# Unused rows of r, k and w at the head of each half, set once on the chip; a dense first v; a newly planned order

## The chip, the core and the metric

The kernel runs on one core of one Trainium2 chip. The metric is device time in microseconds (us) of one execution; the median of several executions is compared. A profile was taken of one execution. Engines: TensorE (PE, weight loads as PEld), VectorE (DVE), ScalarE (ACT), GpSimd (POOL) and SyncE (SP), which issues the transfers.

## The reference

A recurrent attention layer feeds a two-layer product with a gate. Batch 4, 8 heads, 768 tokens, 48 values a head; 2,048 hidden values.

```python
for t in range(S):
    cur = np.einsum('bhd,bhe->bhde', u[None] * kt, vt)
    y[:, :, t] = np.einsum('bhd,bhde->bhe', rt, state + cur)
    state = wt[:, :, :, None] * state + np.einsum('bhd,bhe->bhde', kt, vt)
x = y as (B * S, 384)
h = x @ w_in
g = np.where(h >= 1, h, np.where(h <= -1, 0.0, (h + 1) ** 2 / 4))
out = g @ w_out
```

r, k, v are about 0.1 in size, w lies between 0.8 and 0.95.

## The kernel before, in words

**Attention** works in 12 units of 256 tokens, three for each batch entry, one after the other because a state passes along within an entry. Heads stand in pairs: one pair fills 128 rows, head h in rows 64h to 64h + 47; 16 rows of each half are unused and hold 0 for r and k and 1 for w. They come from DRAM with the rest (`rows` in `layouts`, L982: 128 rows for each load). For each unit `attention` (L384):

- loads w (`wq`, three buffers, 257.5 KB) and r with k (`rk`, three buffers, 512 KB) for two halves q, and v. Units 0 to 3 multiply k by u on chip; later units load r and k also by token (`nk`). A buffer of `rk` is free for the next load when the products of an earlier unit have read it.
- VectorE makes running products of w, forward (`p`, L439) and backward (`y`, L434), two scans each with 514 steps, and multiplies k by y (L468) and r by p (L518).
- TensorE makes the products of r with k among 64 tokens (`among`, L488); VectorE picks the valid part (L494); TensorE transposes k (L527), ScalarE copies it (`kt`, L534); TensorE makes the sums of k and v for each 64 tokens (`umat`, L549); VectorE adds them up into states (L565 to L570); TensorE makes the output of the unit from states and picked products (`cross` and `along`, L598). ScalarE and VectorE write it in two parts as `x`, and for heads that don't fit, six small transfers move rows (L700).
- Unit 0 is handled alone: its v comes from DRAM already spaced to 64 columns a head, into the gate's buffers `g0` and `g1` (256 KB each), and a permutation matrix (`perm`, 192 KB, from DRAM) takes the place of the small transfers.

**Weights** come as 16 packed blocks of 768 KB (`weight`, L343): ScalarE makes one half-word (L363) and the magnitude (L360), GpSimd the other half-word (L364), VectorE puts them together (L366), ScalarE rounds to a first part (L356), VectorE makes the second (L369).

**The two layers** (`products`, L745): for blocks of 512 tokens and each of 16 weight blocks, nine products for h (L952), ScalarE and VectorE for the gate (L763 to L768), nine products for the output (L972). Early steps take 256 tokens.

**The order** of all of it is written out by a planner (`Plan`): each operation has a due time, worked out from tables of numbers (`LEADS`, `DECODES`, `LOADS`, `RAWS`, `SLACK`) and the planner's own costs, and each engine's instructions are emitted in the order that comes out. Where it sees a gap on TensorE it adds products with zeros (`cleared`, L331).

At the start GpSimd sets constants and zeroes buffers (L306 to L318).

Of the kernel before, what the change touches and what calls it, by code (L numbers as in the profile page):

```python
# [13 lines left out]
AF = mybir.ActivationFunctionType  # L14
# [8 lines left out]
NU = NT // UT  # L23
# [25 lines left out]
class Plan:  # L49
# [16 lines left out]
    def __init__(self):  # L66
        self.ops, self.writer, self.readers = [], {}, {}

    def add(self, engine, cost, emit, due, reads=(), writes=(), port=False, size=0, fresh=True, mode=128, spare=0.0):
# [11 lines left out]
        deps.discard(n)  # L81
        self.ops.append(dict(e=engine, cost=cost, emit=emit, due=due, deps=deps, port=port, size=size,
                             fresh=fresh and engine == "PE", touch={*reads, *writes}, mode=mode, spare=spare))
        return n

    def group(self, first, when, lead, loads=0.0):
# [46 lines left out]
    def order(self):  # L133
# [13 lines left out]

        def opened(n):
            op = ops[n]
            since[n] = max((ran[m] if ops[m]["e"] == op["e"] and not ops[m]["size"] else end[m] + self.HOP for m in op["deps"]), default=0.0)  # L150
            open_[op["e"]].append(n)

        def ready(n):
# [62 lines left out]

SLACK = 0.759
LEADS = {0: 384.81, 1: 606.87, 2: 40.05, 3: 27.03, 4: 45.45, 5: 71.8, 6: 60.98, 7: 25.74, 8: 81.18, 9: 211.42, 10: 77.25, 11: 123.12}  # L220
# [12 lines left out]
ALONE = {0}  # L233
INPLACE = {0, 1}
SCALED = {0, 1}
STEP, FIRST, PACED, AFTER = 27.1568, 703.402, 25.4941, 8.52
ROUNDS = 6


def attention_moe(tc, a):  # L240
# [142 lines left out]

    def attention(u, when):  # L384
        if u == EARLY:
            load((when, 40.0), u_sb, a["us"], ["us"])
        first, due = len(plan.ops), None
        third = u % UB
        early = u < EARLY
# [63 lines left out]

        for q in (1, 0):
            s = slot[q]
            if early:
                if u in SCALED:
                    for pr in range(2):
                        op("ACT", 0.42, due, [("k", s), "cst"], [("ku", q), "nk"], lambda q=q, pr=pr: A.activation(
                            ku[:, q, pr * UT : pr * UT + UT], rk[slot[q]][:, 1, pr * UT : pr * UT + UT], AF.Copy,  # L460
                            scale=u_col[:, 2 * q + pr : 2 * q + pr + 1]))
# [515 lines left out]
def layouts(r, k, v, w, u, moe_w_in, moe_w_out):  # L977
# [12 lines left out]
    def tokens(x):  # L990
        return x.transpose(0, 2, 1, 3).reshape(NU, 2, 128, DM).transpose(0, 2, 1, 3)
# [23 lines left out]
    col[:, :D] = u.reshape(4, 2, D).transpose(1, 2, 0)  # L1015
    consts = np.concatenate([eye, two, col.reshape(128, 4)], axis=1)
    v0 = np.pad(tokens(v)[0].reshape(128, 2, H, D), [(0, 0)] * 3 + [(0, HP - D)]).reshape(128, 2, H * HP).transpose(1, 0, 2)
    perm = np.zeros((2, HP, 3, 2, HP), np.float32)
    for j in range(3):
        for h in range(2):  # L1020
            perm[h, 16 * j : 16 * j + 16, j, h, D:] = np.eye(16)
    perm = perm.reshape(128, 3 * 128)
    out = dict(nat=nat, v0=v0, perm=perm, rk=rk, w=rows(wz, 1.0), nk=nk, v=tokens(v), u=ul, wbits=wbits, consts=consts, below=below, us=us)
# [18 lines left out]
```

## Time and profile before

| | us |
|---|---|
| median of 3 runs | 511.38 (510.29 to 512.46) |
| profiled execution | 509.98 |
| its span, first to last instruction | 508.1 |
| TensorE busy | 492.1 |
| VectorE busy | 332.0 |
| ScalarE busy | 295.4 |
| GpSimd busy | 101.1 |

The profiled execution's own time is 1.9 us over its span, and 1.4 us under the median. A busy share is a mean over the whole span; matmuls are pipelined, so a busy TensorE is not TensorE at its peak. The granted clock of TensorE was 0.996 of full speed in the mean.

### The profile page before, as it was taken

How to read it: one execution, taken by the hardware profiler on the slowest of the kernel's cores; microseconds unless marked ns; L12 is line 12 of the kernel's file. 1: busy time of each engine (PE TensorE's matmuls, PEld its weight loads, DVE VectorE, ACT ScalarE, POOL GpSimd, SP SyncE). 2: the span in 40 equal slices, each digit the busy share in tenths (PEclk: the TensorE clock that was granted, in tenths of full speed). 3: DMA queues.
4: the chain of work that ended last, by engine and by line, in shares of the span. 5: the costliest groups of instructions: out<-in, count | busy, mean ns of one | idle time of the engine just before them, and what ended most of it. 6: DMA issues, size and time to landing. Idle time of an engine off the chain costs nothing.

```text
span 508.1 us, 13247 instructions
## 1 busy us (share of the span) xinstructions
PE 492.1 (97%) x5562; PEld 412.2 (81%) x5562; DVE 332.0 (65%) x561; ACT 295.4 (58%) x604; POOL 101.1 (20%) x68
## 2 busy tenths in 40 slices
PE   8999999999999999999999899999999999999994
PEld 7778987889999978888888687888878888888883
DVE  6899997947997799749646888842464333343331
ACT  3588798987876464746534565553463543454440
POOL 2487766801011212111002013000010000000000
PEclk9999999999999999999999999999999999999998
DMA  8974734326742334414006352200110000100001
GB/s 308 404 287 148 276 145 163 115 65 208 219 117 109 126 110 136 162 43 173 23 1 192 106 164 93 89 1 1 63 55 6 17 1 0 64 0 1 0 1 68
DMA packets 21923, 54.13 MB, mean 107 GB/s; under 512 B 3104, under 2 KB 8672, under 8 KB 21856
## 3 DMA queue, kind: packets, MB, share of 16 engines
q1 hardware_dynamic: 21856, 53.21, 30.8%
q8 instruction: 45, 0.74, 0.6%
q14 instruction: 22, 0.18, 0.1%
HBM read 46.32 MB, written 4.72 MB: 100 GB/s over the span
## 4 chain that ended last, share of the span: by engine, by line
PE 76%; DVE 13%; ACT 3%; DMA 3%; issue 3%; SPq 1%; DVEq 0%; ACTq 0%
PE h L952 34%; PE acc L972 33%; PE bank L598 4%; DVE y L434 2%; DVE r L494 2%; PE bank L488 2%; DVE wt L369 2%; DMA rk<-in_rk 1%; DVE p L439 1%; PE bank L527 1%; DMA wq<-in_w 1%; PE bank L549 1%; DVE g L765 1%; DVE gl L768 1%; DVE rk L518 1%
## 5 line engine op out<-in xcount | busy, mean ns | idle before, releaser
L952 PE MATMUL h<-x,wt 128*128 128x512 f32 (+1 forms) x1008 | 216.7, 361 | 1.1 <-DVE g L765 0.7
L952 PEld LDWEIGHTS h<-x,wt 128*128 128x128 f32 x1008 | 168.4, 188 | 30.6 <-DVE g L765 1.1
L972 PE MATMUL acc<-gh,wt 128*128 128x512 f32 (+1 forms) x672 | 151.7, 359 | 0.0
L972 PEld LDWEIGHTS acc<-gh,wt 128*128 128x128 f32 x672 | 113.8, 188 | 19.0
L765 DVE SCALAR_TENSOR_TENSOR g<-g,h 128x512 f32<-128x512 f32 (+1 forms) x112 | 67.4, 605 | 92.1 <-ACT g L764 85.0
L763 ACT ACTIVATE g<-h 128x512 f32<-128x512 f32 (+1 forms) x112 | 59.7, 533 | 85.3 <-PE h L952 84.9
L768 DVE TENSOR_TENSOR gl<-g,gh 128x512 fp32r<-128x512 f32 (+1 forms) x112 | 71.4, 642 | 28.6 <-ACT gh L767 13.4
L767 ACT CAST gh<-g 128x512 fp32r<-128x512 f32 (+1 forms) x112 | 62.1, 557 | 39.3 <-PE acc L972 17.8
L972 PE MATMUL acc<-gl,wt 128*128 128x512 f32 (+1 forms) x336 | 84.1, 357 | 0.0
L972 PEld LDWEIGHTS acc<-gl,wt 128*128 128x128 f32 x336 | 58.4, 187 | 9.8 <-DVE gl L768 0.4
L764 ACT ACTIVATE g<-g 128x512 f32<-128x512 f32 (+1 forms) x112 | 64.0, 571 | 3.2
L364 POOL TENSOR_SCALAR rr<-wraw 128x768 uint16<-128x768 f32 x16 | 52.7, 3293 | 34.8 <-DVE fl L366 17.2
L514 POOL TENSOR_TENSOR r<-cst,d 128x512 f32<-128x512 f32 x16 | 18.0, 1145 | 159.4 <-PE bank L598 134.0
L506 POOL TENSOR_TENSOR nk<-nk 128x768 f32<-128x768 f32 x8 | 16.9, 2108 | 80.3 <-DMA nk<-in_nk 71.2
L434 DVE TENSOR_TENSOR_SCAN y<-wq,seeds 128x514 f32<-128x514 f32 x24 | 32.2, 1342 | 0.8
L439 DVE TENSOR_TENSOR_SCAN p<-wq,seeds 128x514 f32<-128x514 f32 x24 | 30.2, 1259 | 3.5 <-POOL st L318 2.1
L468 DVE TENSOR_TENSOR rk<-rk,y 128x512 f32<-128x512 f32 x24 | 18.9, 789 | 3.5 <-DMA rk<-in_rk 3.3
L598 PEld LDWEIGHTS bank<-rk,st 48*48 48x48 f32 (+1 forms) x656 | 11.4, 121 | 9.3 <-DVE st L567 4.0
L369 DVE TENSOR_TENSOR wt<-fl,wt 128x768 fp32r<-128x768 f32 x16 | 16.4, 1032 | 3.2 <-ACT wt L356 3.1
L331 PE MATMUL bank<-clear 128*128 128x512 f32 (+1 forms) x57 | 16.8, 411 | 1.6 <-DVE seeds L438 1.6
L363 ACT ACTIVATE rr<-wraw 128x768 uint16<-128x768 uint32 x16 | 17.5, 1094 | 1.1 <-DVE fl L366 1.1
L518 DVE TENSOR_TENSOR rk<-rk,p 128x512 f32<-128x512 f32 x24 | 17.7, 748 | 0.1
(109 smaller groups left out, 384.3 us busy)
## 6 DMA issues: line engine op xcount, KB each, us to landing
rk<-in_rk SPq DMA_DIRECT2D x24, 512.0 KB, 4.8
wraw<-in_wbits SPq DMA_DIRECT2D x16, 768.0 KB, 7.5
wq<-in_w SPq DMA_DIRECT2D x24, 257.5 KB, 3.3
nk<-in_nk SPq DMA_DIRECT2D x8, 768.0 KB, 4.6
vn<-in_v SPq DMA_DIRECT2D x11, 384.0 KB, 5.9
fl<-in_w SPq DMA_DIRECT2D x12, 257.0 KB, 2.8
out_y<-g SPq DMA_DIRECT2D x11, 256.0 KB, 2.3
x<-last SPq DMA_DIRECT2D x66, 32.0 KB, 2.9
```

The costliest lines, as they stand in the source:

```text
L364: op("POOL", 3.35, due, [("raw", f)], ["rr_high"], lambda: G.tensor_scalar(out=r16[:, :, 1], in0=wraw[f][:, :, 1].bitcast(F32), scalar1=0. ...
L369: op("DVE", 0.95, due, [("fl", k), ("wh", f)], [("wl", f)], lambda: V.tensor_tensor(out=w_lo[f], in0=s, in1=w_hi[f].bitcast(F32), op=ALU.s ...
L434: V.tensor_tensor_scan(out=y_[:, ::-1], data0=w[:, SEG:0:-1], data1=sv[:, ::-1], initial=0.0, op0=ALU.mult, op1=ALU.add)
L439: V.tensor_tensor_scan(out=pv[:, q].rearrange("p n c -> p (n c)"), data0=w[:, 0:SEG], data1=sv, initial=0.0, op0=ALU.mult, op1=ALU.add,)
L598: PE.matmul(out=bank[by[g]][HP * half : HP * half + wide, lo : lo + C], start=first, stop=False, skip_group_check=True, **kw)
L763: op("ACT", c, due, [("b", 6 + hk)], [("g", gk)], lambda: nc.scalar.activation(gs, hs, AF.Relu, scale=0.5, bias=0.5))
L764: op("ACT", c, due, (), [("g", gk)], lambda: nc.scalar.activation(gs, gs, AF.Square))
L765: op("DVE", 0.13 + 0.56 * k, due, [("b", 6 + hk)], [("g", gk)], lambda: nc.vector.scalar_tensor_tensor(out=gs, in0=gs, scalar=1.0, in1=hs, ...
L767: op("ACT", c, due, [("g", gk)], [("gh", gk)], lambda: nc.scalar.copy(ghs, gs))
L768: op("DVE", 0.18 + 0.52 * k, due, [("g", gk), ("gh", gk)], [("gl", gk)], lambda: nc.vector.tensor_tensor(out=gls, in0=gs, in1=ghs.bitcast( ...
L952: nc.tensor.matmul(by16(hp, f), lhsT=wx[f][:, cs], rhs=by16(xt[:, j, :], f), start=n == 0, stop=n == 8)
L972: nc.tensor.matmul(by16(o[j]), lhsT=wx[f][:, cs], rhs=by16(gt), start=first and i == 0, stop=stop and i == 2, skip_group_check=True)
```

## The change

The 16 unused rows of each half move to its head: head h now stands in rows 64h + 16 to 64h + 63. For units 0 to 6 the loads of w and of r with k begin at row 16 and have 112 rows (225 and 448 KB); rows 0 to 15 of the buffers are set once on the chip, before the first use (`unread`, `PADS`; the rows 64 to 79 still come with the load). Units 7 to 11 load all 128 rows. Products that read 48 rows of a half or 48 columns of k now take 64. The v of unit 0 comes dense (384 KB) into `vn0` and ScalarE copies it into the spaced `g0` and `g1`, which GpSimd has zeroed. The permutation matrix is made by GpSimd from the identity. The load of u for unit 4 waits for the last weight. All numbers of the order are new.

```diff
+PAD = HP - D
+PADS = [(0, "w", "DVE", (0, 199.0)), (1, "w", "ACT", (0, 190.0)), (0, "k", "POOL", (0, 198.0)), (1, "k", "POOL", (0, 196.0)),
+        (2, "w", "POOL", (0, 194.0)), (2, "k", "POOL", (0, 192.0))]
+WHOLE, MOST, TWO = ((0, 128),), ((PAD, 128),), ((PAD, HP), (HP + PAD, 128))
+CUT = [{"w": MOST, "k": MOST}, {"w": MOST, "k": MOST}, {"w": WHOLE, "k": WHOLE}]
...
-SLACK = 0.759
+SLACK = 1.82
...
+    for c2 in range(2):
+        op("POOL", 0.5, LATER, (), [("g", c2)], lambda c2=c2: G.memset(g_[c2], 0.0))
...
+    def unread(s, what, how, when):
+        t, v, keys = (wq[s], 1.0, [("w", s)]) if what == "w" else (rk[s], 0.0, [("k", s), ("r", s)])
...
+                op(how, 0.55 if what == "w" else 1.04, when, (), [(*keys[0], i)], lambda i=i: e.memset(t[i : i + PAD], v))
...
-            load((when, 40.0), u_sb, a["us"], ["us"])
+            load((when, 40.0), u_sb, a["us"], ["us"], [("wl", NF // 2)])
...
-            load(due, wq[slot[q]], a["w"][u, q], [("w", slot[q])])
-            load(due, rk[slot[q]], a["rk"][u, q], [("k", slot[q]), ("r", slot[q])])
+                cut = CUT[0 if u == 0 else 1 if u <= GUARDED else 2]["w" if t is wq[slot[q]] else "k"]
+                n = None
+                for i, j in cut:
+                    n = load(due, t[i:j], of[i:j], keys, twin=n)
...
-                load(due, g_[c2], a["v0"][c2], [("g", c2)])
-            load(due, perm, a["perm"], ["perm", "nk"])
+                op("ACT", 0.48, due, [("v", 0)], [("g", c2)], lambda c2=c2: A.copy(
+                    g_[c2].rearrange("p (h e) -> p h e", e=HP)[:, :, 0:D], v[:, c2, 0:DM].rearrange("p (h e) -> p h e", e=D)))
+            op("POOL", 0.4, due, (), ["perm", "nk"], lambda: G.memset(perm, 0.0))
+            op("POOL", 0.3, due, ["cst"], ["perm"], lambda: G.tensor_copy(
...
-                            i, o = slice(HP * g, HP * g + HP), slice(HP * h, HP * h + D)
+                            i, o = slice(HP * g, HP * g + HP), slice(HP * h, HP * h + HP)
...
-            i = slice(HP * h, HP * h + D)
+            i = slice(HP * h, HP * h + HP)
```

**SyncE at the start**, before: unit 0's last loads, unit 1's, then the first weight block. (Names end in a buffer's number; `in_wbits` are weights, `wq1`, `wq2`, `rk2`, `vn1` there are unit 1's or 2's.)

```order
L301 DMA rk1_83<-in_rk 128x1024
L301 DMA g0_104<-in_v0 128x512
L301 DMA g1_105<-in_v0 128x512
L301 DMA below0_71<-in_below 128x64
L301 DMA wq2_81<-in_w 128x515
L301 DMA rk2_84<-in_rk 128x1024
L301 DMA vn1_87<-in_v 128x2x384
L301 DMA wq0_79<-in_w 128x515
L351 DMA wraw0_229<-in_wbits 128x1536
```

The same place in the change:

```order
L309 DMA rk1_83<-in_rk 112x1024
L309 DMA vn0_86<-in_v 128x2x384
L309 DMA below0_71<-in_below 128x64
L379 DMA wraw0_206<-in_wbits 128x1536
L309 DMA wq2_81<-in_w 112x515
L309 DMA rk2_84<-in_rk 112x1024
L309 DMA vn1_87<-in_v 128x2x384
L379 DMA wraw1_220<-in_wbits 128x1536
```

The first weight block stands ahead of unit 1's loads, and the second right behind them.

**VectorE in unit 0**, before: from the second k multiply to the first pick (r multiplies L518, scans of unit 1 L439 and L434).

```order
L468 TENSOR_TENSOR rk1_83<-rk1_83,y0_89 128x512
L518 TENSOR_TENSOR rk0_82<-rk0_82,p0_88 128x512
L438 MEMSET seeds0_73 128x2
L439 SCALAR_TENSOR_TENSOR p0_88<-wq2_81,seeds0_73 128x514
L433 RECIPROCAL seeds0_73<-p0_88 128x2
L434 SCALAR_TENSOR_TENSOR y0_89<-wq2_81,seeds0_73 128x514
L518 TENSOR_TENSOR rk1_83<-rk1_83,p0_88 128x512
L438 MEMSET seeds0_73 128x2
L439 SCALAR_TENSOR_TENSOR p0_88<-wq0_79,seeds0_73 128x514
L565 COPY ob0_113<-h1_121 128x4x48
L567 TENSOR_TENSOR ob0_113<-bank2_124,ob0_113 128x4x48
L494 COPY_PREDICATED r0_91<-cst0_67,acc0_117 128x512
```

The same place in the change:

```order
L506 TENSOR_TENSOR rk1_83<-rk1_83,y0_89 128x512
L556 TENSOR_TENSOR rk0_82<-rk0_82,p0_88 128x512
L556 TENSOR_TENSOR rk1_83<-rk1_83,p0_88 128x512
L532 COPY_PREDICATED r0_91<-cst0_67,acc0_117 128x512
L532 COPY_PREDICATED r1_92<-cst0_67,acc1_118 128x512
L475 MEMSET seeds0_73 128x2
L476 SCALAR_TENSOR_TENSOR p0_88<-wq2_81,seeds0_73 128x514
L603 COPY ob0_113<-h1_121 128x4x48
L605 TENSOR_TENSOR ob0_113<-bank2_124,ob0_113 128x4x48
L605 TENSOR_TENSOR g2_106<-h1_121,ob0_113 128x4x48
L532 COPY_PREDICATED r0_91<-below0_71,acc2_119 128x512
L394 SCALAR_TENSOR_TENSOR fl0_114<-fl0_114,rr0_116 128x768
```

Unit 0's two r multiplies and its first picks stand ahead of unit 1's first scan; unit 1's second scan and the first scan of its other half are moved behind the state adds, and the first weight is put together there (L394).

**SyncE ahead of unit 8**, before (`rk2` is unit 8's second half, `rk0` unit 9's first, `x1` the small transfers of units 6 and 7):

```order
L700 DMA x1_102<-last0_103 16x2x256 x4
L301 DMA wq1_80<-in_w 128x515
L301 DMA wq2_81<-in_w 128x515
L301 DMA rk0_82<-in_rk 128x1024
L301 DMA vn1_87<-in_v 128x2x384
L301 DMA rk2_84<-in_rk 128x1024
L700 DMA x1_102<-last0_103 16x2x256 x6
```

The same place in the change:

```order
L738 DMA x1_102<-last0_103 16x2x256 x6
L309 DMA wq1_80<-in_w 128x515
L309 DMA wq2_81<-in_w 128x515
L309 DMA nk0_85<-in_nk 128x1536
L309 DMA rk2_84<-in_rk 128x1024
L309 DMA rk0_82<-in_rk 128x1024
L309 DMA vn1_87<-in_v 128x2x384
L738 DMA x1_102<-last0_103 16x2x256 x6
```

Unit 8's `rk2` stands ahead of unit 9's `rk0` and of the v load.

## Rows read from the trace of the kernel before

**Rows 1.** The page's part 1: busy time, share of the span, instructions of each engine.
```profile
PE 492.1 (97%) x5562; PEld 412.2 (81%) x5562; DVE 332.0 (65%) x561; ACT 295.4 (58%) x604; POOL 101.1 (20%) x68
```

**Rows 2.** Stretches: length, busy PE, PEld, DVE, ACT, POOL, clock, DMA share, GB/s.
```profile
12.00:14.00 2.00, 2.00 (x69) 1.77 (x70) 1.93 (x3) 0.19 (x1) 0.00 (x0) 1.00 1.07 426
...
40.00:60.00 20.00, 19.01 (x362) 17.41 (x363) 19.85 (x31) 15.70 (x35) 16.77 (x8) 1.00 0.69 245
60.00:80.00 20.00, 19.66 (x155) 16.91 (x157) 19.69 (x32) 18.60 (x34) 10.56 (x5) 1.00 0.43 158
...
180.00:200.00 20.00, 19.28 (x273) 15.86 (x272) 19.16 (x31) 10.60 (x25) 5.24 (x3) 1.00 0.44 146
...
250.00:300.00 50.00, 48.04 (x689) 38.17 (x688) 32.36 (x57) 24.84 (x53) 6.50 (x5) 1.00 0.31 103
```

**Rows 3.** VectorE's timeline: start, length, what, idle time before and its releaser.
```profile
3.62 1.23 DVE L439 TENSOR_TENSOR_SCAN p<-wq,seeds 128x514 f32<-128x514 f32 x1 [2.09 <-POOL st L318]
...
10.73 0.69 DVE L518 TENSOR_TENSOR rk<-rk,p 128x512 f32<-128x512 f32 x1
...
11.84 1.23 DVE L439 TENSOR_TENSOR_SCAN p<-wq,seeds 128x514 f32<-128x514 f32 x1 [0.40 <-DMA wq<-in_w]
...
14.45 0.67 DVE L518 TENSOR_TENSOR rk<-rk,p 128x512 f32<-128x512 f32 x1
...
17.03 1.36 DVE L494 COPY_PREDICATED r<-cst,acc 128x512 f32<-128x512 int32 x2
...
22.28 0.96 DVE L369 TENSOR_TENSOR wt<-fl,wt 128x768 fp32r<-128x768 f32 x1 [0.90 <-ACT wt L356]
24.57 0.96 DVE L366 SCALAR_TENSOR_TENSOR fl<-fl,rr 128x768 int32<-128x768 int32 x1 [1.33 <-POOL rr L364]
...
35.18 0.40 DVE L765 SCALAR_TENSOR_TENSOR g<-g,h 128x256 f32<-128x256 f32 x1
```

**Rows 4.** The same view, GpSimd and TensorE.
```profile
0.87 0.53 POOL L306 MEMSET seeds<- 128x514 f32 x1
...
16.73 3.06 POOL L364 TENSOR_SCALAR rr<-wraw 128x768 uint16<-128x768 f32 x1 [13.17 <-DMA wraw<-in_wbits]
...
25.61 3.56 POOL L364 TENSOR_SCALAR rr<-wraw 128x768 uint16<-128x768 f32 x1 [1.08 <-DVE fl L366]
...
27.04 1.57 PE L952 MATMUL h<-x,wt 128*128 128x256 f32 x9
```

**Rows 5.** The same view near 184 us: GpSimd and VectorE side by side.
```profile
183.77 2.08 POOL L506 TENSOR_TENSOR nk<-nk 128x768 f32<-128x768 f32 x1 [10.08 <-DMA nk<-in_nk]
...
184.27 2.66 DVE L434 TENSOR_TENSOR_SCAN y<-wq,seeds 128x514 f32<-128x514 f32 x1
```

**Rows 6.** Around unit 8: chain (start, length), timeline, and a stretch as in rows 2.
```profile
265.70 1.56 PE bank L598 x96
...
267.95 7.52 DMA rk<-in_rk
...
266.14 0.33 SPq L301 DMA_DIRECT2D rk<-in_rk  x1
...
278.77 2.31 DVE L518 TENSOR_TENSOR rk<-rk,p 128x512 f32<-128x512 f32 x1
...
280.00:282.00 2.00, 0.87 (x57) 0.87 (x60) 1.95 (x3) 0.00 (x0) 0.53 (x1) 1.00 0.46 133
```

**Rows 7.** Chain: products of L488; stretches, PE alone: L549, then L598 (64 and 48 wide).
```profile
302.54 1.09 PE bank L488 x64
...
184.00:185.20 1.20, 0.94 (x64) 1.00 0.01 3
...
41.00:44.00 3.00, 1.63 (x96) 1.00 0.39 79
86.00:88.00 2.00, 1.56 (x96) 1.00 0.17 37
```

**Rows 8.** Timeline of SyncE's issues: the loads ahead of unit 9.
```profile
294.97 0.82 SPq L301 DMA_DIRECT2D rk<-in_rk  x2
```

More of the change, by code (lines that the diff above doesn't have):

```diff
@@ L67, in __init__, with add @@
         self.ops, self.writer, self.readers = [], {}, {}
-    def add(self, engine, cost, emit, due, reads=(), writes=(), port=False, size=0, fresh=True, mode=128, spare=0.0):
+    def add(self, engine, cost, emit, due, reads=(), writes=(), port=False, size=0, fresh=True, mode=128, spare=0.0, twin=None):
         deps = {self.writer[x] for x in (*reads, *writes) if x in self.writer}
@@ L81, in add @@
         deps.discard(n)
+        if twin is not None:
+            deps = {*self.ops[twin]["deps"], twin}
         self.ops.append(dict(e=engine, cost=cost, emit=emit, due=due, deps=deps, port=port, size=size,
-                             fresh=fresh and engine == "PE", touch={*reads, *writes}, mode=mode, spare=spare))
+                             fresh=fresh and engine == "PE", touch={*reads, *writes}, mode=mode, spare=spare, twin=twin))
         return n
@@ L149, in opened @@
             op = ops[n]
-            since[n] = max((ran[m] if ops[m]["e"] == op["e"] and not ops[m]["size"] else end[m] + self.HOP for m in op["deps"]), default=0.0)
+            since[n] = max((ran[m] if ops[m]["e"] == op["e"] and (not ops[m]["size"] or op["twin"] == m) else end[m] + self.HOP for m in op["deps"]), default=0.0)
             open_[op["e"]].append(n)
@@ L235 @@
 SCALED = {0, 1}
-STEP, FIRST, PACED, AFTER = 27.1568, 703.402, 25.4941, 8.52
+STEP, FIRST, PACED, AFTER = 27.1568, 703.402, 25.4941, 8.254
 ROUNDS = 6
@@ L307, in attention_moe @@
     op("POOL", 0.1, SOON, (), ["seeds"], lambda: G.memset(seeds[:, :, 0], 1.0))
+    LATER = 0, 150.0
     for i in range(2):
-        op("POOL", 0.1, SOON, (), [("vpad", i)], lambda i=i: G.memset(vn[i][:, :, DM:], 0.0))
+        op("POOL", 0.1, LATER, (), [("vpad", i)], lambda i=i: G.memset(vn[i][:, :, DM:], 0.0))
     for h in range(2):
-        op("POOL", 0.5, SOON, (), [("R", h)], lambda h=h: G.memset(r_[h], 0.0))
-    op("POOL", 0.5, SOON, (), ["ob", ("s", "ob0"), ("s", "ob1")], lambda: G.memset(ob, 0.0))
-    op("POOL", 0.5, SOON, (), [("g", 2), ("s", "g2")], lambda: G.memset(g_[2][:, 0:256], 0.0))
+        op("POOL", 0.5, LATER, (), [("R", h)], lambda h=h: G.memset(r_[h], 0.0))
+    op("POOL", 0.5, LATER, (), ["ob", ("s", "ob0"), ("s", "ob1")], lambda: G.memset(ob, 0.0))
+    op("POOL", 0.5, LATER, (), [("g", 2), ("s", "g2")], lambda: G.memset(g_[2][:, 0:256], 0.0))
+    for c2 in range(2):
+        op("POOL", 0.5, LATER, (), [("g", c2)], lambda c2=c2: G.memset(g_[c2], 0.0))
     wide_st = {"ob0": ob[:, 0:256], "ob1": ob[:, 256:512], "g2": g_[2][:, 0:256]}
@@ L317, in attention_moe @@
     for i in range(STATES):
-        op("POOL", 0.1, SOON, (), [("spad", i)], lambda i=i: G.memset(st[i][:, 4 * D :], 0.0))
+        op("POOL", 0.1, LATER, (), [("spad", i)], lambda i=i: G.memset(st[i][:, 4 * D :], 0.0))
     op("DVE", 0.2, SOON, ["zero"], ["clear"], lambda: V.tensor_copy(clear, zero))
+    def unread(s, what, how, when):
+        t, v, keys = (wq[s], 1.0, [("w", s)]) if what == "w" else (rk[s], 0.0, [("k", s), ("r", s)])
+        cut = CUT[0 if s < 2 else 1][what]
+        for i in (0, HP):
+            if cut is WHOLE or i and cut is MOST:
+                continue
+            if how == "ACT":
+                op(how, 0.6 if what == "w" else 1.0, when, ["zero"], [(*keys[0], i)], lambda i=i: A.activation(
+                    t[i : i + PAD], zero[i : i + PAD, 0:1].broadcast_to([PAD, t.shape[1]]), AF.Copy, bias=v))
+            else:
+                e = V if how == "DVE" else G
+                op(how, 0.55 if what == "w" else 1.04, when, (), [(*keys[0], i)], lambda i=i: e.memset(t[i : i + PAD], v))
+    for s, what, how, when in PADS:
+        unread(s, what, how, when)
     def warm():
@@ L412, in attention @@
         for q in (1, 0):
-            load(due, wq[slot[q]], a["w"][u, q], [("w", slot[q])])
-            load(due, rk[slot[q]], a["rk"][u, q], [("k", slot[q]), ("r", slot[q])])
+            for t, of, keys in ((wq[slot[q]], a["w"][u, q], [("w", slot[q])]),
+                                (rk[slot[q]], a["rk"][u, q], [("k", slot[q]), ("r", slot[q])])):
+                cut = CUT[0 if u == 0 else 1 if u <= GUARDED else 2]["w" if t is wq[slot[q]] else "k"]
+                n = None
+                for i, j in cut:
+                    n = load(due, t[i:j], of[i:j], keys, twin=n)
         if u == 0:
@@ L421, in attention @@
         if alone:
+            load(due, v[:, :, 0:DM], a["v"][u], [("v", 0)])
             for c2 in range(2):
-                load(due, g_[c2], a["v0"][c2], [("g", c2)])
-            load(due, perm, a["perm"], ["perm", "nk"])
+                op("ACT", 0.48, due, [("v", 0)], [("g", c2)], lambda c2=c2: A.copy(
+                    g_[c2].rearrange("p (h e) -> p h e", e=HP)[:, :, 0:D], v[:, c2, 0:DM].rearrange("p (h e) -> p h e", e=D)))
+            op("POOL", 0.4, due, (), ["perm", "nk"], lambda: G.memset(perm, 0.0))
+            op("POOL", 0.3, due, ["cst"], ["perm"], lambda: G.tensor_copy(
+                perm.rearrange("p (j h e) -> p j h e", j=3, h=2)[:, :, :, D:],
+                ident.rearrange("p (h e) -> p h e", h=2)[:, :, 0:D].rearrange("p h (j i) -> p j h i", j=3)))
         else:
@@ L455, in attention @@
             s = slot[q]
+            wpad, kpad = ([(t, s, i) for i in (0, HP)] for t in "wk")
             if early:
@@ L458, in attention @@
                     for pr in range(2):
[L459 removed]
+                        op("ACT", 0.42, due, [("k", s), "cst", *kpad], [("ku", q), "nk"], lambda q=q, pr=pr: A.activation(
                             ku[:, q, pr * UT : pr * UT + UT], rk[slot[q]][:, 1, pr * UT : pr * UT + UT], AF.Copy,
@@ L462, in attention @@
                 else:
-                    op("POOL", 2.6, due, [("k", s), "cst"], [("ku", q), "nk"], lambda q=q: with_u(q))
-            op("DVE", 1.34, due, [("w", s)], [("p", q), "seeds"], lambda q=q: scan(q, False), port=True)
+                    op("POOL", 2.6, due, [("k", s), "cst", *kpad], [("ku", q), "nk"], lambda q=q: with_u(q))
+            op("DVE", 1.34, due, [("w", s), *wpad], [("p", q), "seeds"], lambda q=q: scan(q, False), port=True)
             op("ACT", 0.2, due, [("p", q)], [("ptot", u, q)], lambda q=q: A.copy(
@@ L496, in picked @@
                 data=bank[of].rearrange("p (n c) -> p n c", c=C))
-        both = [("r", slot[0]), ("r", slot[1])]
+        both = [("r", slot[0]), ("r", slot[1]), *(("k", slot[q], i) for q in range(2) for i in (0, HP))]
         if early:
@@ L517, in attention @@
         for q in (1, 0):
-            op("DVE", 0.69, due, [("p", q)], [("r", slot[q])], lambda q=q: V.tensor_tensor(
+            op("DVE", 0.69, due, [("p", q), *(("k", slot[q], i) for i in (0, HP))], [("r", slot[q])], lambda q=q: V.tensor_tensor(
                 out=parts(q, 0), in0=parts(q, 0), in1=pv[:, q, :, 0:UT], op=ALU.mult), port=True)
@@ L982, in rows @@
     def rows(x, fill):
-        return np.pad(x, [(0, 0)] * 3 + [(0, HP - D), (0, 0)], constant_values=fill).reshape(NU, 2, 128, x.shape[-1])
+        return np.pad(x, [(0, 0)] * 3 + [(PAD, 0), (0, 0)], constant_values=fill).reshape(NU, 2, 128, x.shape[-1])
     rk = rows(np.concatenate([dt(r), dt(k)], axis=-1), 0.0).reshape(NU, 2, 128, 2, 2 * UT)
@@ L1014, in layouts @@
     col = np.zeros((2, HP, 4), np.float32)
-    col[:, :D] = u.reshape(4, 2, D).transpose(1, 2, 0)
+    col[:, PAD:] = u.reshape(4, 2, D).transpose(1, 2, 0)
     consts = np.concatenate([eye, two, col.reshape(128, 4)], axis=1)
[L1017 to L1023, printed above, removed]
+    out = dict(nat=nat, rk=rk, w=rows(wz, 1.0), nk=nk, v=tokens(v), u=ul, wbits=wbits, consts=consts, below=below, us=us)
     return {n: np.ascontiguousarray(x) for n, x in out.items()}
```

10 lines of the change are left out of this document (5 added, 5 removed).

## The prediction

> **What bounds the kernel now.** I read four views in this order. The page says that TensorE is busy for 492.1 of 508.1 us and VectorE for 332.0 [rows 1]. That share is an average over two stages, so the table by stretches comes next [rows 2]: from 40 to 80 us VectorE has no gap (19.85 and 19.69 of 20 us) while TensorE, with clearing products in its waits, is at 19.01 and 19.66. From 250 to 300 it is VectorE that idles (32.36 of 50). So **early, VectorE sets the pace; later, TensorE does**, and only its gaps can be won there: 0.72 us in 180 to 200 and 1.96 us in 250 to 300 [rows 2]. Third, the timelines of the engines show where the early pace is lost [rows 3, 4]; fourth, the chain and the timeline around 267 to 282 us show why TensorE stands there [rows 6].
>
> **The early stage: the new order on VectorE.** Between the start of unit 0's first r multiply (10.73) and the second gate (35.18) VectorE is idle in three places [rows 3]: 0.40 us for the w load of unit 1, 0.90 us for ScalarE's cast of the first weight, 1.33 us for GpSimd's half of the second weight. Together 2.63 us; the rest is work. The change does the same work there in another order.
> - The w load of unit 1 is needed after both r multiplies and both picks instead of after one multiply: one multiply (0.67) and two picks (1.36) later, about 13.3 instead of 11.8. That wait goes.
> - Weight 0 is issued behind unit 0's loads alone. By the shapes, 4,552 KB are queued up to and including it before; now 2,628 KB (w 225 and r/k 448 KB per half, v 384, constants 98, mask 32, weight 768). Of the difference 1,411 KB are unit 1's loads, which now stand behind it, and 513 KB are rows no longer sent. At the 426 GB/s of the stretch from 12 to 14 us [rows 2] this is some 4.6 us, so GpSimd's half can start near 12 us instead of 16.73 [rows 4]. VectorE needs it after 3.06 us more, at 15, and comes to it (scan, three state adds, a pick) at about 16.4. Then a scan stands between combining weight 0 and its second use: ScalarE's cast is covered. GpSimd's half of weight 1 starts when VectorE has combined weight 0 (17.4), ends near 20.5, and is wanted at 22.5: covered too.
> - What is late next: GpSimd's half of weight 2 starts after weight 1 is combined (23.4), takes 3.06 to 3.56 us [rows 4] and is wanted at 26.1, so some 0.4 us of wait stay.
>
> That is 2.63 - 0.4 = 2.2 us. I take **1.8**, since a VectorE instruction beside a GpSimd one that reads is sometimes longer (a scan 1.23 alone [rows 3], 2.66 beside one [rows 5]). Low end 0. High end 3.9: TensorE's own chain for unit 0 gets shorter by about that, because the second r multiply ends at 11.9 instead of 15.1 [rows 3], and the picks and ScalarE's copies behind it follow; the first product (27.04 [rows 4]) would start near 23.2. But the second product needs weight 1, and VectorE gives it at about 33.1 by the same walk, so TensorE cannot keep that lead. From the gates on, both orders list nearly the same VectorE work, without a gap until 80 us, so the 1.8 us are kept; the clearing products that are dropped or added stand in TensorE's waits for VectorE and cost nothing while it is the bound.
>
> **Added instructions at the start.** VectorE sets one w pad (0.5 us by the 0.53 of a memset of the same row length [rows 4]) before its first scan at 3.62, in a wait of 2.09 us [rows 3]: nothing. ScalarE sets another after its table load and is then idle: nothing. ScalarE copies unit 0's v into the spaced tile, two copies near 9 and 10 us, before the second kt copy, which waits for VectorE's second k multiply and which unit 0's state product waits for: nothing. GpSimd sets four pads and the permutation first; its memsets, which end just before VectorE's first scan now (that wait was for them [rows 3]), then run until about 9 us (3,586 elements of pads are 3.7 us at 0.53 per 514, the permutation 0.7, two more full tiles 1.0). The k pads are done at about 4.1, before r/k of unit 0 land. What they could do to VectorE is a rival below. The u load moved behind the last weight is first needed by unit 4: nothing.
>
> **The later stage: unit 8.** The along products of unit 7 end at 267.3. Unit 8's second r/k load is issued at 267.95, behind unit 9's r/k (266.14) and a v load, takes 7.52 us, and VectorE then does the r multiply beside GpSimd's nk multiply in 2.31 us [rows 6] instead of 0.67 [rows 3]. TensorE has six groups of nine products (12.2 us) between; it is busy for only 0.87 of the 2 us to 282 [rows 6], and the rest of the 1.96 us [rows 2] lies around that and before the same unit's later products. In the new order of SyncE unit 8's load comes first, and TensorE has eleven groups between (22.4 us), longer than the 14.7 us from 267.3 to 282.0. I take **1.9 us** gained, low end 0, high end 1.96.
>
> **Other units.** From unit 5 on the spacings change in both directions: unit 5 has six groups before its products instead of four (its stall is the 0.72 us), unit 6 three instead of seven, units 9 and 10 more, 11 the same. I set this at 0, with 0.8 us either way.
>
> **Wider state products.** Their weights get 64 columns instead of 48, 64 products a unit, and this counts from unit 2 on, where TensorE is the bound. Below: 0, since 48 columns still pass through. Above: products of 64 columns either way take 1.09 us for 64 against 0.94 [rows 7], 0.15 us a unit, 1.5 in all. Nearest row: the output products with weights 64 wide against 48 wide, 1.63 against 1.56 us for 96 [rows 7], so 0.05 for 64, **0.5 us** in ten units. The later w, r and k loads of units 2 to 6 are an eighth smaller; nobody on the path waits for them: 0.
>
> **Sum.** -1.8 - 1.9 + 0.5 = -3.2 us. The profiled execution took 510.0 us (span 508.1 and 1.9 around it), so it becomes 506.8; the median shown is 511.4, so I predict **508.2 us**, 0.63% less. A difference of 0.5% (2.6 us: below 508.8, above 513.9) is about what a measurement of this kernel can tell from no change.
>
> **Rivals.**
> - *The lead is given back (510.0).* GpSimd is busy for 16.77 of 20 us from 40 to 60 [rows 2]; if its decodes become the bound, 0.3 of the 1.8 us stays: -0.3 - 1.9 + 0.5 = -1.7 us. For it: the wait left at weight 2. Against: GpSimd's waits are mostly for VectorE, which is earlier.
> - *All gaps go (506.9).* 1.8, 1.96 and the 0.72 of unit 5 [rows 2], the wider products free: -4.5 us. Against: each gap is a chance meeting of engines, and a new order has its own.
> - *Slower: unit 6 stands (514.8).* TensorE has three groups (6.1 us) between unit 5's products and unit 6's, which need a load that waits for unit 5. If this load took what unit 8's took before (14.7 us until TensorE could go on), TensorE would stand for 8 us, or 6.6 with the 1.4 us of products of unit 5 and turns in between: 511.4 - 3.2 + 6.6. It decides as soon as more than about 7 us pass. Against: unit 9 has the same three groups now, its load issued in front of the others (294.97 [rows 8]), and its products start at 302.54 [rows 7] without a wait; unit 6's load stands in front, too.
> - *Slower: the memsets hold VectorE (513.9).* GpSimd's memsets now lie beside unit 0's four scans (3.6 to 9.8 us); before, they were over when the first began, so no row has the pair. If each scan took 2.66 instead of 1.23 us, as one did at 184.27 beside GpSimd's multiply (183.77) [rows 5], that is 5.7 us. It decides from 0.8 us a scan. Against: that partner reads its tiles, a memset reads nothing. [...]
> - *Fewer rows, no shorter loads (508.7).* A load of 112 rows could take as long as one of 128; no row shows one. Then 193 KB of the 1,924 KB ahead of weight 0 are not won, 0.5 us of GpSimd's start, which had 1.4 us to spare, and I count 0.5 us at most. [...]
>
> **Chances.** Forecast 0.46, lead given back 0.20, all gaps 0.13, unit 6 0.07, memsets 0.06, loads no shorter 0.08. The forecast alone, by its bounds of about 1 us each way, is 506.8 to 509.6. The range 505.0 to 512.6 leaves out the two slower cases and little of the fastest. Faster by over 0.5%: three quarters of the forecast (0.35), all gaps (0.13), half of the last (0.04) and a little of the first rival, 0.53; slower 0.10; the same 0.37.
>
> **What the next profile would show.** Right: weight 0's GpSimd half near 12 us; first product near 23 us; second gate near 33.4; VectorE's scans at 1.23 in the first 10 us; no TensorE gap of 1 us before unit 8; state products still about 0.94 us for 64. Wrong: scans over 2 us beside memsets, GpSimd without gaps from 25 to 60 us, or a TensorE gap of several us at unit 6, about 210 us.

## The result, and the profile after

| | before | after |
|---|---|---|
| median of the comparison, us | 511.54 (510.29 to 512.46) | 517.34 (516.21 to 519.01) |
| profiled execution, us | 509.98 | 516.21 |
| its span, us | 508.1 | 513.9 |

The ratio is 1.0125, with a 95% interval of 1.0089 to 1.0161: **5.8 us slower**, where 3.2 us faster was forecast, and outside the range of 505.0 to 512.6.

The page's first part, against [rows 1]: TensorE is busy for 3.1 us more.

```profile
PE 495.2 (96%) x5556; PEld 416.1 (81%) x5556; DVE 328.3 (64%) x562; ACT 297.5 (58%) x607; POOL 101.5 (20%) x76
```

The table by stretches of the kernel after, columns as in [rows 2]; 20 to 25 and 28 to 36 us were not shown there.

```profile
12.00:14.00 2.00, 1.82 (x122) 1.83 (x125) 1.35 (x5) 0.90 (x2) 0.79 (x1) 1.00 1.08 318
20.00:25.00 5.00, 5.00 (x77) 4.23 (x67) 4.34 (x6) 4.77 (x11) 3.03 (x2) 1.00 1.05 325
28.00:36.00 8.00, 6.97 (x135) 5.70 (x136) 5.10 (x7) 4.19 (x8) 5.01 (x3) 0.57 1.03 278
...
180.00:200.00 20.00, 20.00 (x285) 16.86 (x284) 15.59 (x29) 12.08 (x27) 3.90 (x3) 1.00 0.44 139
250.00:300.00 50.00, 50.00 (x578) 40.63 (x577) 28.85 (x51) 25.79 (x54) 6.00 (x5) 1.00 0.30 100
```

So these two of the kernel before:

```profile
20.00:25.00 5.00, 4.91 (x110) 4.14 (x109) 2.73 (x5) 3.59 (x8) 3.08 (x1) 1.00 1.04 401
28.00:36.00 8.00, 7.49 (x166) 6.45 (x165) 7.95 (x16) 7.06 (x14) 7.51 (x4) 1.00 0.79 293
```

Read the last three columns first: clock, share of the transfer engines, GB/s. From 12 to 14 us the transfer engines are as busy as before (1.08 against 1.07) and move 318 GB/s instead of 426; from 20 to 25 us 325 instead of 401. From 28 to 36 us VectorE, which sets the early pace, works for 5.10 us of 8; before, it had no gap there (7.95). The granted clock in that stretch is 0.57. In the late stage TensorE has no gap left from 250 to 300 us, as was forecast for unit 8, and none from 180 to 200 either.

VectorE's timeline, columns as in [rows 3]:

```profile
3.77 1.23 DVE L476 TENSOR_TENSOR_SCAN p<-wq,seeds 128x514 f32<-128x514 f32 x1 [1.88 <-POOL rk L345]
...
8.60 1.23 DVE L471 TENSOR_TENSOR_SCAN y<-wq,seeds 128x514 f32<-128x514 f32 x1
...
13.95 1.26 DVE L476 TENSOR_TENSOR_SCAN p<-wq,seeds 128x514 f32<-128x514 f32 x1 [0.65 <-DMA wq<-in_w]
...
24.56 0.90 DVE L506 TENSOR_TENSOR rk<-rk,y 128x512 f32<-128x512 f32 x1 [0.61 <-ACT nk L497]
...
29.34 0.69 DVE L506 TENSOR_TENSOR rk<-rk,y 128x512 f32<-128x512 f32 x1 [2.55 <-ACT nk L497]
...
36.00 0.72 DVE L532 COPY_PREDICATED r<-below,bank 128x512 f32<-128x512 int32 x1 [1.46 <-PE bank L526]
...
51.13 0.41 DVE L803 SCALAR_TENSOR_TENSOR g<-g,h 128x256 f32<-128x256 f32 x1
```

The last row is a **mark**: it is the fourth gate of the execution. In the kernel before, VectorE has done the same set of operations ahead of its fourth gate (the change adds one memset of a pad), and there that gate begins 4.4 us earlier.

```profile
46.72 0.41 DVE L765 SCALAR_TENSOR_TENSOR g<-g,h 128x256 f32<-128x256 f32 x1
```

GpSimd and TensorE after, the same view:

```profile
8.58 0.34 POOL L330 MEMSET st<- 128x16 f32 x6
13.21 3.09 POOL L392 TENSOR_SCALAR rr<-wraw 128x768 uint16<-128x768 f32 x1 [4.29 <-DMA wraw<-in_wbits]
...
25.32 1.22 PE L990 MATMUL h<-x,wt 128*128 128x256 f32 x8 [0.25 <-ACT x L689]
26.37 0.52 PE L359 MATMUL bank<-clear 128*128 128x512 f32 x2
28.96 1.99 PE L526 MATMUL bank<-rk,nk 64*64 64x64 f32 x64 [2.08 <-ACT nk L497]
30.88 3.57 PE L359 MATMUL bank<-clear 128*128 128x512 f32 x8
```

And the chain of waits after (start, length, what), from the start of that wait, and two places further on:

```profile
19.91 8.47 DMA rk<-in_rk
28.41 0.52 ACT nk L497
28.96 1.99 PE bank L526 x64
...
288.45 1.08 PE bank L587 x64
...
333.24 7.64 DMA rk<-in_rk
```

Unit 1's second r/k load is issued at 19.91 and lands at 28.4. ScalarE's multiply by u (L497) waits for it, VectorE's k multiply and TensorE's r·k products wait for that. TensorE stands for 2.1 us, and afterwards the granted clock is low: 64 products take 1.99 us at 28.96 where 64 take 1.09 in [rows 7], and eight clearing products 3.57.

The page's part on transfers gives a median time from issue to landing: 5.3 us for the 14 short r/k loads and 4.8 for the 10 whole ones. This alone proves nothing about the rows, since the short loads are the early ones in a full queue; whether they take longer needs a test.

### The profile page after: what moved, and what is told of

It reads as the page before. It is cut to its first block, busy times and chain, and to the rows that moved or that the text cites. A ratio compares the mean times of both kernels' runs of the same rounds, so it can differ in the third digit from the quotient of the medians.

```text
span 513.9 us, 13230 instructions
## 1 busy us (share of the span) xinstructions
PE 495.2 (96%) x5556; PEld 416.1 (81%) x5556; DVE 328.3 (64%) x562; ACT 297.5 (58%) x607; POOL 101.5 (20%) x76
## 4 chain that ended last, share of the span: by engine, by line
PE 78%; DMA 5%; POOL 5%; issue 4%; DVE 4%; ACT 3%; SPq 1%; POOLq 0%; DVEq 0%; ACTq 0%
PE h L990 33%; PE acc L1010 33%; PE bank L636 4%; POOL rr L392 4%; DMA rk<-in_rk 3%; PE bank L526 3%; PE bank L587 2%; DMA wq<-in_w 2%; PE bank L565 2%; DVE y L471 1%; PE bank L359 1%; POOL nk L487 1%; SPq L309 1%; ACT fl L388 1%; DVE p L476 0%
## 5 line engine op out<-in xcount | busy, mean ns | idle before, releaser
L392 POOL TENSOR_SCALAR rr<-wraw 128x768 uint16<-128x768 f32 x16 | 51.5, 3217 | 37.1 <-DVE fl L394 30.2
L544 POOL TENSOR_TENSOR nk<-nk 128x768 f32<-128x768 f32 x8 | 14.7, 1831 | 116.8 <-DMA nk<-in_nk 81.2
L506 DVE TENSOR_TENSOR rk<-rk,y 128x512 f32<-128x512 f32 x24 | 17.7, 737 | 7.4 <-DMA rk<-in_rk 4.0
L572 ACT COPY kt<-bank 128x512 f32<-128x512 f32 x24 | 13.4, 584 | 14.0 <-PE bank L565 14.0
L532 DVE COPY_PREDICATED r<-below,bank 128x512 f32<-128x512 int32 x22 | 15.3, 730 | 4.0 <-PE bank L526 4.0
L823 ACT COPY g<-acc 128x512 f32<-128x512 f32 (+1 forms) x12 | 6.3, 571 | 19.7 <-PE acc L1010 19.5
```

Source lines behind the costliest of these rows:

```text
L392: op("POOL", 3.35, due, [("raw", f)], ["rr_high"], lambda: G.tensor_scalar(out=r16[:, :, 1], in0=wraw[f][:, :, 1].bitcast(F32), scalar1=0. ...
```

## The experiments

**Theory:** the loads of 112 rows hold the transfer engines longer than loads of 128 rows, the start's queue runs late, and the rest follows from it. **Rivals:** the new order is bad in itself; the wider state products; the clock; the setting of the pads. Each median is set against the kernel before in the same session (509.96, 510.19 and 510.53 us in the three).

### The new order with whole loads, and with 48 columns

All numbers of the order stay; `do` is what a load really sends, and the pads are not set.

```diff
-                    n = load(due, t[i:j], of[i:j], keys, twin=n)
+                    n = load(due, t[i:j], of[i:j], keys, do=(t, of), twin=n)
...
-                op(how, 0.55 if what == "w" else 1.04, when, (), [(*keys[0], i)], lambda i=i: e.memset(t[i : i + PAD], v))
+                op(how, 0.55 if what == "w" else 1.04, when, (), [(*keys[0], i)], lambda: None)
```

> The changed kernel in its own order, but units 0 to 6 load all 128 rows again (the unused rows come from DRAM) and no pad is set on the chip. Loads theory (a load of 112 rows holds the transfer engines longer for each byte, so unit 1's r/k comes late, VectorE waits, TensorE falls to half clock): the rate from 12 to 20 us goes from 301 to 369 back to about 400 GB/s, unit 1's second r/k load lands within 7 us instead of 8.5, the granted clock stays 1.00 from 25 to 40 us, and the time falls by 4 to 5 us to about 512.5. Order theory (weights ahead of unit 1's loads make it late whatever the rows): no change, 516.5 to 518. Both keep 1.08 us for 64 of the wider state products.

The second kernel also moves the unused rows back to the tail, lets the state products read 48 columns of k and the products with the state 48 rows:

```diff
-                            i, o = slice(HP * g, HP * g + HP), slice(HP * h, HP * h + HP)
+                            i, o = slice(HP * g, HP * g + HP), slice(HP * h, HP * h + D)
...
-            i = slice(HP * h, HP * h + HP)
+            i = slice(HP * h, HP * h + D)
```

> As the one before, and the unused rows are back at the tail of each half, so that the state products have weights of 48 columns and the products with the state read 48 rows. Wider-products theory: the state products go from 1.08 to 0.94 us for 64, and ten to twelve units make the time 1.4 to 1.7 us lower than with all rows at the head. If other gaps take that up: the same within 0.5 us. With the loads theory the time is then near 511, with the order theory near 515.5.

Whole loads: 508.39 us, ratio 0.9966 (0.9949 to 0.9983). With 48 columns: 505.53 us, ratio 0.9909 (0.988 to 0.9937). Against the kernel after (1.0125) whole loads take off some 8 us where 4 to 5 were expected, and 48 columns 2.9 us more where 1.4 to 1.7 were. The stretches with whole loads:

```profile
12.00:14.00 2.00, 2.00 (x129) 1.93 (x129) 1.43 (x4) 1.05 (x2) 0.99 (x1) 1.00 1.06 417
20.00:25.00 5.00, 4.68 (x31) 3.95 (x31) 4.52 (x8) 4.41 (x11) 2.55 (x2) 1.00 1.01 401
28.00:36.00 8.00, 6.73 (x157) 5.64 (x156) 7.95 (x13) 4.88 (x8) 5.20 (x3) 1.00 0.67 256
```

Its VectorE at the k multiply that had waited for 2.55 us, and at the mark:

```profile
26.32 0.69 DVE L506 TENSOR_TENSOR rk<-rk,y 128x512 f32<-128x512 f32 x1
...
45.51 0.41 DVE L803 SCALAR_TENSOR_TENSOR g<-g,h 128x256 f32<-128x256 f32 x1
```

More bytes, and everything is earlier: the rates are those of the kernel before, the wait is gone, VectorE has no gap, the clock stays at 1.00, the mark is 5.6 us ahead of the kernel after and 1.2 us ahead of the kernel before. **The order is good; the short loads cost it.** The setting of the pads went together with the short loads here. What it costs can be seen at VectorE's first scan, which waits for a pad until 3.77 us in the kernel after and starts at 3.59 us without pads, 0.2 us.

The groups of instructions by shape (count, busy us, mean ns) price the wider state products. With 64 columns:

```profile
L587 PE MATMUL bank<-vn,kt 64*64 64x48 f32 x704 | 12.6, 220 | 0.4 <-ACT kt L572 0.4
...
L587 PE MATMUL h<-g,kt 64*64 64x48 f32 x32 | 1.1, 219 | 0.2 <-ACT kt L572 0.2
L587 PE MATMUL bank<-g,kt 64*64 64x48 f32 x32 | 1.1, 220 | 0.0
```

With 48 columns:

```profile
L587 PE MATMUL bank<-vn,kt 64*48 64x48 f32 x704 | 10.3, 207 | 0.3 <-ACT kt L572 0.3
...
L587 PE MATMUL h<-g,kt 64*48 64x48 f32 x32 | 0.9, 206 | 0.2 <-ACT kt L572 0.2
L587 PE MATMUL bank<-g,kt 64*48 64x48 f32 x32 | 0.9, 207 | 0.0
```

The last two groups of each run side by side (both between 11.9 and 13.1 us), so they count once: 13.7 us against 11.2, which is 2.5 of the 2.9 us between the two medians. TensorE's busy time as a whole falls by as much, from 491.4 to 488.8 us. The products with the state are no part of it: 592 of them take 13.3 us with 64 rows and with 48.

### The old order with short loads

The loads of w likewise; head rows, pads and 64-wide state products come with it.

```diff
-            load(due, rk[slot[q]], a["rk"][u, q], [("k", slot[q]), ("r", slot[q])])
+            load(due, rk[slot[q]], a["rk"][u, q], [("k", slot[q]), ("r", slot[q])], do=(rk[slot[q]][16:128], a["rk"][u, q][16:128]) if u <= GUARDED else None)
```

> The kernel before in its own order, with only this of the change: unused rows at the head, units 0 to 6 load 112 rows, pads set on the chip, state products 64 wide. Loads theory: slower than before by 1.5 us (wider products) and 2 to 4 us more for late loads, 515 to 517, with 300 to 370 GB/s from 10 to 20 us instead of 386 to 426. Order theory: slower by the wider products alone, 513, with the rate of before.

517.73 us, ratio 1.0142 (1.0102 to 1.0182): the old order loses as well, at the same low rates, and somewhat more than expected. Its stretches:

```profile
12.00:14.00 2.00, 1.91 (x69) 1.49 (x68) 1.38 (x2) 0.63 (x2) 0.00 (x0) 1.00 1.11 309
20.00:25.00 5.00, 5.00 (x129) 4.40 (x130) 3.61 (x6) 3.30 (x8) 3.53 (x2) 1.00 1.07 312
```

### Twelve more clearing products in the wait

```diff
-        halves = int(FILLED * us / ZEROS * 2)
+        halves = int(FILLED * us / ZEROS * 2) + (24 if len(met) == 7 else 0)
+        met.append(us)
```

> The changed kernel with twelve more clearing products on TensorE ahead of unit 1's first products of r with k (where it stood idle from 26.9 to 29.0 us), and nothing else. Clock theory (the fall of the granted clock to 0.50 from 28.5 to 35.8 us costs time by itself, since the products that VectorE waits for take twice as long there): the clock stays 1.00 and the time falls by 1.5 to 2.5 us to about 515.3. If VectorE and the loads set the pace alone: the clock stays 1.00 and the time stays at 517 within 0.7.

517.12 us, ratio 1.0139 (1.0101 to 1.0178): nothing gained in the median. The profiled execution was the shortest of the five (513.31 us; the others 516.85 to 518.29). In it the clock did not fall:

```profile
28.00:36.00 8.00, 7.14 (x150) 5.73 (x148) 4.87 (x8) 4.19 (x8) 3.52 (x3) 1.00 1.03 266
```

VectorE idles there as it does after the change (4.87 against 5.10 us busy), and its mark comes at 50.46, only 0.7 us before 51.13. So the fallen clock is a consequence and, by this profile, a small part of the early loss. Of the 3.0 us between the two spans (510.9 and 513.9) the rest lies behind the mark; 1.3 us of it is a gap of TensorE from 346 to 350 us that this profile lacks (5.00 of 5 us busy from 345 to 350). The four longer executions had mean clocks of 0.988 to 0.993, against 0.996 in the profiled one; what the clock costs in those is not settled by this.

### Transfers alone

```python
kinds = [("r128", "rk", [(0, 128)]), ("r112h", "rk", [(16, 128)]), ("r112t", "rk", [(0, 112)]), ("r96", "rk", [(0, 96)]),
         ("r48x2", "rk", [(16, 64), (80, 128)]), ("w128", "w", [(0, 128)]), ("w112h", "w", [(16, 128)])]
```

> Transfers alone: six loads in a row of each kind, each kind beginning when the one before has landed. Rows of 4,096 bytes: 128 rows; 112 rows from row 16; 112 rows from row 0; 96 rows from row 0; two loads of 48 rows each (rows 16 to 63 and 80 to 127). Rows of 2,060 bytes: 128 rows, 112 rows from row 16. The layers and the attention are left out. Loads theory: 128 rows about 400 GB/s, 112 rows from row 16 a fifth or more below that, so that the six loads take as long as or longer than six of 128 rows. If the place of the first row causes it, 112 rows from row 0 are at the full rate; if the count does, they are as slow. Rival: all kinds within 5% in GB/s, and the slow rate of the changed kernel comes from what else is in the queue.

The kernel leaves out the layers and the attention. VectorE copies a bit of each load as it lands, so in the steady part of a stage the distance between two such rows is the time of a load. The last of 128 rows, then of rows 16 to 127, then of rows 0 to 111:

```profile
10.46 0.30 DVE L125 COPY seen<-r 16x1 f32<-16x1 f32 x2 [0.99 <-DMA r<-in_rk]
11.72 0.31 DVE L125 COPY seen<-r 16x1 f32<-16x1 f32 x2 [0.96 <-DMA r<-in_rk]
...
23.67 0.30 DVE L125 COPY seen<-r112h 16x1 f32<-16x1 f32 x2 [1.35 <-DMA r112h<-in_rk]
25.32 0.30 DVE L125 COPY seen<-r112h 16x1 f32<-16x1 f32 x2 [1.34 <-DMA r112h<-in_rk]
...
37.05 0.31 DVE L125 COPY seen<-r112t 16x1 f32<-16x1 f32 x2 [1.32 <-DMA r112t<-in_rk]
38.66 0.31 DVE L125 COPY seen<-r112t 16x1 f32<-16x1 f32 x2 [1.30 <-DMA r112t<-in_rk]
```

512 KB take 1.26 us (416 GB/s), 448 KB take 1.65 (278 GB/s) or 1.61. An eighth less data takes 28 to 31% longer, whether the rows begin at 0 or at 16. The transfer engines are busy all the same: their share is 1.05 from 22 to 25 us, at 280 GB/s. One early distance in each of these three stages is 0.5 us or more longer than the others; from the first landing to the sixth it is 7.8 us with 128 rows, 8.9 and 8.3 with 112.

The other stages: rows 0 to 95 take 1.36 to 1.51 us, and two loads of 48 rows 0.93 us each. Six loads of w take 4.7 us from the first landing to the sixth with 128 rows and 4.6 with 112, so there an eighth less data saves next to nothing. The kernels here always shorten w together with r and k; how the loss divides between them stays open.

### Which of the loads cost the time

First short loads in units 2 to 6 alone, whole ones in 0 and 1 (against the kernel with whole loads; no pads are set):

```diff
-                    n = load(due, t[i:j], of[i:j], keys, do=(t, of), twin=n)
+                    n = load(due, t[i:j], of[i:j], keys, do=(t, of) if u < 2 else None, twin=n)
```

> The changed kernel in its own order; units 0 and 1 load all 128 rows, units 2 to 6 load 112, no pad is set on the chip. If the harm lies in the start (the 16 loads of units 0 and 1 delay the whole queue up to unit 1's last load): as with all rows loaded, about 0.997 of before. If it lies in the loads of units 2 and 3, which share the transfer engines with unit 1's last load and the weights from 8 to 40 us: most of the loss stays, 1.008 to 1.012 of before.

Then the reverse, with the pads set:

```diff
-                    n = load(due, t[i:j], of[i:j], keys, do=(t, of), twin=n)
+                    n = load(due, t[i:j], of[i:j], keys, do=None if u < 2 else (t, of), twin=n)
```

> The counterpart: units 0 and 1 load 112 rows, with the pads set on the chip, units 2 to 6 load all 128. Start theory: 1.010 to 1.0125 of before. Later-loads theory: about 1.000 of before. If the loss is shared out by the bytes in each part, both this and the one before lie near 1.004.

And the kernel after, unchanged, beside them:

> The changed kernel once more, on the same chip as the next two. 1.0125 of before, about 517.

512.27 us (ratio 1.0042, 1.0015 to 1.0069), 513.77 (1.0065, 1.0044 to 1.0085) and 516.88 (1.0114, 1.0085 to 1.0142). Against whole loads (0.9966, from the session before) that is 0.0076, 0.0099 and 0.0148 of some 510 us: 3.9, 5.0 and 7.5 us, each uncertain by some 1.5 us. Both parts cost, so neither the start alone nor the later loads alone is the cause; whether together they cost less than the sum of 8.9 us is not clear of the noise. In the profiles the mark tells when:

| kernel | mark, us | behind whole loads |
|---|---|---|
| whole loads | 45.51 | |
| short in units 0 and 1 | 49.25 | 3.7 |
| short in units 2 to 6 | 49.53 | 4.0 |
| after, with more clearing products | 50.46 | 4.9 |
| after | 51.13 | 5.6 |
| after, again | 52.19 | 6.7 |

The loads of unit 2 stand in the start's queue as well. By the mark, 5.6 of the 7.4 us between the spans of the kernel after and of the one with whole loads (513.9 and 506.5) are lost. The wait that carries it stands in the second profile of the kernel after, too: the k multiply waits for 3.06 us there.

### Why 112 rows take longer

```python
kinds = [("full", "rk", [(0, 128)]), ("low", "rk", [(0, 64)]), ("mid", "rk", [(32, 96)]), ("most", "rk", [(16, 128)]),
         ("near", "rk", [(0, 120)])]
```

> Transfers alone: the layers and the attention are left out, the output is not computed. Five stages of six r/k loads, each read by VectorE as it lands: all 128 rows (512 KB), rows 0 to 63 (256 KB), rows 32 to 95 (256 KB), rows 16 to 127 (448 KB), rows 0 to 119 (480 KB). In the transfers alone before, 128 rows landed every 1.26 us and 112 rows every 1.65 us. [...] Theory B, a load of fewer rows is slow by its row count alone: both 64-row loads alike, near 1.0 to 1.25 us as the 48-row loads (0.93 us) scaled by rows. [...]

VectorE's copies again:

```profile
9.61 0.30 DVE L125 COPY seen<-full 16x1 f32<-16x1 f32 x2 [0.97 <-DMA full<-in_rk]
10.89 0.31 DVE L125 COPY seen<-full 16x1 f32<-16x1 f32 x2 [0.97 <-DMA full<-in_rk]
...
18.48 0.30 DVE L125 COPY seen<-low 16x1 f32<-16x1 f32 x2 [0.97 <-DMA low<-in_rk]
19.74 0.30 DVE L125 COPY seen<-low 16x1 f32<-16x1 f32 x2 [0.96 <-DMA low<-in_rk]
...
32.04 0.30 DVE L125 COPY seen<-mid 16x1 f32<-16x1 f32 x2 [0.34 <-DMA mid<-in_rk]
32.65 0.32 DVE L125 COPY seen<-mid 16x1 f32<-16x1 f32 x2 [0.31 <-DMA mid<-in_rk]
...
58.16 0.30 DVE L125 COPY seen<-near 16x1 f32<-16x1 f32 x2 [1.89 <-DMA near<-in_rk]
60.35 0.31 DVE L125 COPY seen<-near 16x1 f32<-16x1 f32 x2 [1.89 <-DMA near<-in_rk]
```

Again these are distances of the steady part. 128 rows: 1.28 us. Rows 0 to 63: 1.26 us, for half the bytes. Rows 32 to 95, the same bytes: 0.61 us. Rows 0 to 119: 2.19 us. So the row count alone (theory B) does not set the time: which rows are sent does, by a factor of two between the two loads of 64 rows (1.26 against 0.61 us; from the first landing to the sixth 6.2 and 4.8 us). Nor does the time follow the count upward: 112 rows take 1.65 us, 120 take 2.19 and 128 take 1.28. What it is in the rows that sets the time, no run here shows: **that short loads take longer is shown, why they do is not.**

### The best version again

The new order with whole loads and 48 columns:

> The new order with all 128 rows sent, unused rows back at the tail and 48 columns in the state products, again, with more rounds. Our theory (the order gains, the short loads lose): 0.990 to 0.993 of the kernel before, some 4 to 5 us less. Rival (the first session flattered it): 0.996 or more.

506.45 us, ratio 0.9914 (0.9889 to 0.9938): **it beats both kernels**, by 4.1 us the one before, in two sessions alike.

## Why the prediction was wrong

**The step that failed** is the price of the short loads, in three places. "At the 426 GB/s of the stretch from 12 to 14 us [rows 2] this is some 4.6 us" carries the rate of whole loads over to short ones. "The later w, r and k loads of units 2 to 6 are an eighth smaller; nobody on the path waits for them: 0" puts the rest at nothing. And the rival that a load of 112 rows "could take as long as one of 128" was counted at 0.5 us at most: it was bounded by equality on one side, though no row of before showed such a load and nothing excluded a longer one. Instead an r/k load of 112 rows takes 1.65 us where one of 128 takes 1.26, unit 1's second load became a wait of 2.55 us on VectorE, short loads in units 2 to 6 alone cost 3.9 us, and all of them together 7.5 us.

By its other steps:

- *Early stage, -1.8 us.* Right in kind, and the size was near. With whole loads the mark is 1.2 us ahead of before; with short loads 4.4 behind. Weight 0's GpSimd half came at 13.2 (forecast: near 12) from 16.73 [rows 4]; the first product at 24.8 and, with whole loads, 24.0 (forecast 23), from 27.04. The second gate, forecast at 33.4, came at 44.7, and at 39.1 with whole loads: it stands behind more work in the new order, so it was no fit place to read the gain.
- *Unit 8, -1.9 us.* Right: 50.00 of 50 us busy, against 48.04 [rows 2]; TensorE did not stand at unit 6 either (20.00 of 20 us in each stretch from 180 to 240).
- *Wider state products, +0.5 us.* Mis-sized: 2.5 us. The nearest row was taken, the output products with weights 64 wide against 48 [rows 7]. The upper bound of 0.15 us a unit was too low as well, since it set the chain's 1.09 us against a busy time of 0.94. In the chain, 64 products with 48 columns take 0.86 us before, and with 64 columns 1.08 at 288.45, so 0.22 us a unit:

```profile
308.32 0.86 PE bank L549 x64
```

- *Memsets.* That rival fell: scans beside memsets, which end at 8.9, took 1.23 us as they did alone. The first scan began 0.15 us later than before, behind a pad that was priced at nothing.
- *Lead given back.* The lead was lost, to the loads and not to GpSimd's decodes.
- *Others, 0 ± 0.8 us.* A new wait of the same kind as unit 8's stands at 333.24: a load of 7.64 us and 1.27 us of TensorE idle from 346 to 350. In the second profile of the same kernel only 0.22 us are idle from 340 to 350, so this is no fixed cost.
- *Smaller slips,* which decided nothing: of the 513 KB called rows no longer sent, only some 193 KB are such rows, the rest is the permutation matrix and the denser v; by its own terms the lead given back ends at 509.7 us instead of 510.0, TensorE would stand for 8.6 us instead of 8 at unit 6, and the second r multiply ends at 12.1 instead of 11.9.

The sum over the parts: -1.2 (early) -1.9 (unit 8) +2.5 (wider products) +7.5 (short loads) = +6.9 us, against +5.8 measured in the first comparison and +6.7 in the second (516.88 and 510.19). The first two are read from single profiles, and the parts do not fit to better than about 1 us: without the short loads they give -0.6, where the kernel with whole loads gained 1.6 (508.39 and 509.96).

## What to carry to other kernels

Sending fewer rows does not by itself make a transfer shorter (here 448 KB took 1.65 us where 512 KB took 1.26): compare GB/s beside the share of the transfer engines, and time a load of the new shape alone before planning a queue full of them. Where a change joins an order and a new shape, run the order with the old shape: here it held a gain of 4 us that the loads and 16 more columns had hidden. An unknown with no row of its kind has to be bounded on both sides, and its price looked for behind it in the queue: here it came due at unit 1's second load, which landed 8.5 us after its issue.

## What the runs showed of the hardware

- The transfer time of r/k rows: 128 rows 1.26 to 1.28 us, rows 16 to 127 1.65, rows 0 to 111 1.61, rows 0 to 119 2.19, rows 0 to 95 1.36 to 1.51, rows 0 to 63 1.26, rows 32 to 95 0.61 (each in a queue of six like loads, in the steady part).
- A state product with 48 moving columns takes 220 ns in the mean with weights of 64 columns and 207 with 48, though the same columns pass through; in the chain 64 of them take 1.08 and 0.86 us.
- After TensorE had been idle for 2.1 us (26.9 to 28.96), the granted clock was 0.57 from 28 to 36 us, and 0.50 from 30 to 34. With clearing products in that place it was 1.00 in the profiled execution.
